# A third buffer for cast q, one input buffer fewer, and a new split of one ReLU stage

## The chip, the cores and the metric

The kernel runs on one core of a Trainium2 chip. The core has a matrix engine (TensorE, PE in the profile), a vector engine (VectorE, DVE), a scalar engine (ScalarE, ACT), a general engine (GpSimd, POOL), and a sync engine (SyncE, SP), which here only issues DMA transfers. Each engine works off its own queue in order; engines wait for one another through semaphores. PEld is TensorE's loading of weights, which runs beside its matmuls. The metric is the time of one execution on the device in microseconds (us), lower is better. Where several runs are given, the median is meant.

## The reference

The input is q, k, v of 4 batches, 8 heads, 768 positions and 64 numbers per head. Two layers follow each other. The first is a linear attention with a decaying state; the second mixes by two Fourier transforms, normalizes, and applies a two-layer ReLU network:

```python
for t in range(S):
    state = gamma * state + outer(k[:, :, t], v[:, :, t])
    y[:, :, t] = scale * q[:, :, t] @ state
X = fft(fft(x, axis=1), axis=2)
u = x + real(X)
un = (u - mean(u)) / sqrt(var(u) + 1e-6)
out = u + relu(un @ w_ch1) @ w_ch2     # 512 -> 2048 -> 512
```

Here x is y with its heads side by side: 768 rows of 512 numbers for each batch.

## The kernel before

**Attention.** Heads go in pairs, and the four pairs of a batch are taken in turn as i = 0 to 3 (the list `PAIR_ORDER` says which heads these are). `load_unit` issues three loads per pair from SP, for q, k and v, each into one tile of the pool `inp`, which has 11 buffers (line 159 is the load). A load into a buffer that has been used waits until that buffer's last reader is done. `cast_unit` turns them to 16 bits. In batches 0 and 1 q is cast by POOL into the first half of a padded buffer `q16z`, and TensorE transposes it. In batches 2 and 3 (`b >= NPE`) ACT casts q with two copies (line 374), one for each head of the pair, into `q16z`, whose other places hold zeros; then SP issues a DMA transpose of the whole buffer into `qTz` (line 541), beside another of k into `kT` (line 543). Two buffers `q16z` are used in turn, `qzs[i % 2]`: a cast for pair i has to wait until the transpose of the pair that last used that buffer has landed. POOL casts k and v (lines 376 and 381) in all batches. `pad_unit` writes the zeros of `q16z` on DVE during batch 1's attention (lines 253 and 254). After the transposes come the products of q and k (`wkA`, line 593, masked on DVE, line 596), those of k and v (`wkK`, line 612, and the running state `s`, lines 618 and 622), and y (`wkY`, lines 643 and 647), which ACT scales into `x` (line 655).

**Mixing.** The Fourier transforms are matmuls with tables of sines and cosines. Their last step is `s2_unit`, once for each block `kb` of 128 rows, six in a batch. It is a chain over four engines: TensorE makes `pq` (line 826), ACT copies two parts of it into `qn` (lines 828 and 829), DVE makes the two halves of `u` (lines 833 and 836), POOL adds `x` to both (lines 863 and 865), DVE takes the statistics (lines 882 and 883), and ACT makes `un` (line 884). `un` is transposed into `unT`, in the later batches by DMA (line 909).

**The network.** For each half `rt` of a batch's rows (384 rows, three blocks), `h_unit` makes 16 blocks `fb` of the hidden layer: four matmuls into one PSUM buffer `psh` (line 929), which ACT (line 933) or DVE (line 935) then empties into `ht` with a ReLU. The list `ACT_ROWS` says for each half which blocks ACT empties. Afterwards `ch_unit` makes the output: 16 matmuls for each 128 rows into `psc` (line 972), one DVE instruction (line 976) and a store from SP (line 980). `psh` and `psc` share one PSUM pool with three buffers, so the matmuls of block fb can start only when block fb-3 has been emptied.

**The order.** The network of batch b is written interleaved with the attention of batch b+1 and with the mixing of the second half of batch b and of the first half of batch b+1: `emit` sorts all these units by due times. Blocks kb 3 to 5 of a batch's mixing therefore fall into the first ReLU stage of the same batch. The order of the first batch is pinned by hand. Behind that, a scheduler in the kernel framework puts each engine's instructions in line, by what it takes to be ready, and inserts the waits that the buffers need; it may put an instruction that is written later ahead of one written earlier on the same engine.

Of the kernel before, what the change touches and what calls it, by code (L numbers as in the profile page):

```python
# [14 lines left out]
f16 = mybir.dt.float16  # L15
# [3 lines left out]
P = 128  # L19
B, H, S, D = 4, 8, 768, 64  # L20
DM = 512
DFF = 2048
NCH = S // P
# [7 lines left out]
ON_ACT = {'q': (0, 1, 0), 'kv': (1, 1, 1), 'g': (0, 1, 1), 'gr': (0, 0, 0)}  # L31
FB = 1
NPE = 2
ACT_ROWS = ((2, 4, 5, 6, 7, 8, 9, 10, 14), (0, 3, 6, 7, 9, 10, 11, 12, 14, 15))


@with_exitstack
def kernel(
# [13 lines left out]
    def pool(name, bufs, **kw):  # L52
        return ctx.enter_context(tc.tile_pool(name=name, bufs=bufs, **kw))

    const = pool("const", 1)
    inp = pool("inp", 11)
    vp = pool("vp", 4)
    kp = pool("kp", 3)
    tp = pool("tp", 2)
# [189 lines left out]
                                scalar2=1.0, op0=ALU.mult, op1=ALU.mult)  # L249

    def pad_unit():
        for j in range(2):
            nc.vector.memset(qzs[j][:, 0, :, D:P], 0.0)
            nc.vector.memset(qzs[j][:, 1, :, 0:D], 0.0)

# [65 lines left out]
        return run  # L321


    xts, qns, qzs, qts = [], [], [], []
    for j in range(2):
        x = const.tile([P, NCH, 2, XW], f16, tag=f"x16_{j}", name=f"x16_{j}")
        xts.append(x)
        qz = const.tile([P, 2, NCH, P], f16, tag=f"q16z_{j}", name=f"q16z_{j}")
        qzs.append(qz)
        qt = const.tile([P, 2, NCH, P], f16, tag=f"qTz_{j}", name=f"qTz_{j}")  # L330
        qts.append(qt)
        t = const.tile([P, 257], f32, tag=f"qn_{j}", name=f"qn_{j}", padded_shape=[P, 260])
        nc.gpsimd.memset(t[:, 0:257:256], 0.0)
        qns.append(t)
# [18 lines left out]
    at, q16_of, kd_of, v16_of, last_cast = {}, {}, {}, {}, {}  # L353

    def cast_unit(b, i):
        def run():
            h0 = 2 * PAIR_ORDER[i]
            q32, k32, v32 = (in_of.pop((n, b, i)) for n in "qkv")
            kd = kp.tile([P, NCH, 2, D], f16, tag="kd16", name="kd16")
            v16 = vp.tile([P, NCH, 2, D], f16, tag="v16", name="v16")  # L360
            with ExitStack() as es:
                if b < NPE:
                    if (b, i - 1) in last_cast:
                        es.enter_context(tc.issue_after(last_cast[b, i - 1].ins))
                    q16 = qzs[i % 2].rearrange("p h c d -> p (h c d)")[
                        :, 0:NCH * P].rearrange("p (c h d) -> p c h d", c=NCH, h=2)
                    es.enter_context(tc.issue_after(nc.gpsimd.tensor_scalar(
                        out=q16, in0=q32.rearrange("p h c d -> p c h d"), scalar1=1.0,
                        scalar2=1.0, op0=ALU.mult, op1=ALU.mult).ins))
                else:  # L370
                    q16 = qzs[i % 2]
                    for h2 in range(2):
                        dst = q16[:, h2, :, D * h2:D * h2 + D]
                        nc.scalar.copy(dst, q32[:, h2])
                for h2 in range(2):
                    kc = nc.gpsimd.tensor_scalar(out=kd[:, :, h2, :], in0=k32[:, h2],  # L376
                                                 scalar1=gkd[:, h0 + h2:h0 + h2 + 1],
                                                 scalar2=1.0, op0=ALU.mult, op1=ALU.mult)
                    if b < NPE:
                        es.enter_context(tc.issue_after(kc.ins))  # L380
                last_cast[b, i] = nc.gpsimd.tensor_scalar(  # L381
                    out=v16, in0=v32.rearrange("p h c d -> p c h d"), scalar1=1.0, scalar2=1.0,
                    op0=ALU.mult, op1=ALU.mult)
            q16_of[b, i], kd_of[b, i], v16_of[b, i] = q16, kd, v16
        return run

    def q0_unit(i):
        def run():
            q16 = q16_of[0, i] = qzs[i % 2].rearrange("p h c d -> p (h c d)")[
                :, 0:NCH * P].rearrange("p (c h d) -> p c h d", c=NCH, h=2)  # L390
            nc.gpsimd.tensor_scalar(out=q16, in0=in_of.pop(("q", 0, i)).rearrange(
                "p h c d -> p c h d"), scalar1=1.0, scalar2=1.0, op0=ALU.mult, op1=ALU.mult)
        return run
# [530 lines left out]
    def h_unit(b, rt, fb):  # L924
        def run():
            unT = lb[b]["unT"]
            psh = ps_pm.tile([P, 384], f32, tag="pm", name="psh", padded_shape=[P, DM])
            for cb in range(4):
                nc.tensor.matmul(psh, w116[:, cb, fb * P:(fb + 1) * P],  # L929
                                 unT[:, cb, rt * 384:(rt + 1) * 384],  # L930
                                 start=(cb == 0), stop=(cb == 3))
            if fb in ACT_ROWS[rt]:
                nc.scalar.activation(ht16[:, fb, :], psh, AF.Relu, bias=0.0, scale=-1.0)  # L933
            else:
                nc.vector.tensor_scalar(out=ht16[:, fb, :], in0=psh, scalar1=-1.0, scalar2=0.0,  # L935
                                        op0=ALU.mult, op1=ALU.max)
        return run
# [239 lines left out]
```

## Time and profile before

| | |
|---|---|
| median of 5 runs | 248.72 us (248.57 to 251.57) |
| the profiled execution: time on the device | 248.6 us |
| its span, first instruction to last | 246.6 us |
| TensorE matmul busy | 234.4 us, 95% of the span |
| DVE busy | 176.4 us, 72% |
| ACT busy | 130.6 us, 53% |
| POOL busy | 73.3 us, 30% |
| granted TensorE clock | 1.0 |

The profile records one execution. Busy time is the time in which an engine had an instruction under way; the rest of the span it stood idle. The timeline lists an engine's instructions in order of time, with the start and the length in us, instructions of one kind that follow each other merged (x3 means three), and in brackets the idle time ahead of an instruction and who ended it. The list of waits adds such idle times up by who waited for whom. "To landing" is the time from the issue of a DMA to the arrival of its last byte. The span and the 2.0 us around it make up the 248.6 us.

### The profile page before, as it was taken

How to read it: one execution, taken by the hardware profiler on the slowest of the kernel's cores; microseconds unless marked ns; L12 is line 12 of the kernel's file. 1: busy time of each engine (PE TensorE's matmuls, PEld its weight loads, DVE VectorE, ACT ScalarE, POOL GpSimd, SP SyncE). 2: the span in 40 equal slices, each digit the busy share in tenths (PEclk: the TensorE clock that was granted, in tenths of full speed). 3: DMA queues.
4: the chain of work that ended last, by engine and by line, in shares of the span. 5: the costliest groups of instructions: out<-in, count | busy, mean ns of one | idle time of the engine just before them, and what ended most of it. 6: DMA issues, size and time to landing. Idle time of an engine off the chain costs nothing.

```text
span 246.6 us, 5310 instructions
## 1 busy us (share of the span) xinstructions
PE 234.4 (95%) x2024; PEld 144.4 (59%) x2024; DVE 176.4 (72%) x427; ACT 130.6 (53%) x295; POOL 73.3 (30%) x130
## 2 busy tenths in 40 slices
PE   6998899999999999999999999799999998999994
PEld 2455578856775645765567456465666455545543
DVE  8998957898788786996985739687895656424112
ACT  8798678487786447862248427742247317202500
POOL 6667500395500074650001707520002304000000
PEclk9999999999999999999999999999999999999999
DMA  8999999799999288989999579494200241221012
GB/s 179 261 256 145 203 196 205 171 247 254 278 214 213 51 170 196 197 151 143 239 272 219 105 168 202 100 148 114 84 1 0 49 148 21 45 85 43 0 45 85
DMA packets 99209, 36.39 MB, mean 148 GB/s; under 512 B 89840, under 2 KB 96240, under 8 KB 99184
## 3 DMA queue, kind: packets, MB, share of 16 engines
q1 hardware_dynamic: 94960, 31.86, 62.6%
q0 software_dynamic: 4224, 4.19, 10.7%
q8 instruction: 16, 0.26, 0.5%
q14 instruction: 9, 0.07, 0.1%
HBM read 27.26 MB, written 6.29 MB: 136 GB/s over the span
## 4 chain that ended last, share of the span: by engine, by line
PE 72%; ACT 9%; DVE 5%; DMA 4%; SPq 3%; POOL 3%; issue 2%; ACTq 0%; DVEq 0%
PE psc L972 30%; PE psh L929 24%; PE ps L729 3%; SPq L159 3%; PE psh L946 3%; PE wkA L593 3%; DMA k<-in_k_dram 2%; DMA qTz<-q16z 2%; PE wkY L647 2%; ACT un L884 1%; PE wkY L643 1%; PE wkK L612 1%; PE pq L826 1%; POOL u L865 1%; DVE bst L882 1%
## 5 line engine op out<-in xcount | busy, mean ns | idle before, releaser
L972 PE MATMUL psc<-w,ht 128*128 128x512 f16 (+1 forms) x400 | 89.8, 371 | 0.0
L929 PE MATMUL psh<-unT,w 128*128 128x384 f16 x448 | 82.1, 326 | 2.4 <-ACT ht L933 2.3
L972 PEld LDWEIGHTS <-ht 128*128 128x128 f16 x400 | 38.0, 98 | 35.0
L929 PEld LDWEIGHTS <-w 128*128 128x128 f16 x448 | 42.2, 98 | 26.2 <-issue 3.4
L933 ACT ACTIVATE ht<-psh 128x384 f16<-128x384 f32 x67 | 31.9, 489 | 37.2 <-PE psh L929 36.2
L863 POOL TENSOR_TENSOR u<-u,x 128x256 f32<-128x256 f32 x21 | 13.3, 635 | 110.5 <-DVE u L833 100.1
L976 DVE SCALAR_TENSOR_TENSOR ob<-psc,stats,u 128x512 f32<-128x512 f32 (+1 forms) x25 | 18.0, 721 | 26.2 <-PE psc L972 26.1
L935 DVE TENSOR_SCALAR ht<-psh 128x384 f16<-128x384 f32 x45 | 24.7, 550 | 8.7 <-PE psh L929 8.2
L596 DVE TENSOR_TENSOR atm<-wkA,maskp 128x512 f16<-128x512 f32 x36 | 23.9, 682 | 1.0 <-PE wkA L593 1.0
L884 ACT ACTIVATE un<-u,stats 128x512 f16<-128x512 f32 x21 | 15.2, 723 | 15.2 <-DVE stats L883 10.9
L882 DVE BATCH_NORM_STATS2 bst<-u 128x6 f32<-128x512 f32 x21 | 14.6, 694 | 8.9 <-POOL u L865 8.8
L622 DVE SCALAR_TENSOR_TENSOR s<-s,gk,wkK 128x128 f16<-128x128 f16 x48 | 16.4, 342 | 2.5 <-ACT s L618 1.4
L655 ACT ACTIVATE x<-wkY,gexp 128x384 f16<-128x384 f32 x24 | 12.9, 584 | 8.3 <-PE wkY L647 8.3
L145 PE MATMUL wps<-ht 128*128 128x512 f16 x40 | 13.5, 444 | 2.2 <-POOL ht L196 2.2
L376 POOL TENSOR_SCALAR kd<-k,gexp 128x384 f16<-128x384 f32 x24 | 13.8, 588 | 2.2 <-DMA k<-in_k_dram 2.2
L865 POOL TENSOR_TENSOR u<-u,x 128x256 f32<-128x256 f32 x21 | 13.3, 636 | 3.6 <-DVE stats L883 1.8
L593 PE MATMUL wkA<-qTz,kT 128*128 128x256 f16 x72 | 13.6, 273 | 0.1
L828 ACT COPY qn<-pq 128x128 f32<-128x128 f32 x18 | 4.9, 273 | 12.9 <-PE pq L826 12.9
L946 PE MATMUL psh<-unT,w 128*128 128x128 f16 x192 | 11.5, 219 | 0.1
L946 PEld LDWEIGHTS <-w 128*128 128x128 f16 x192 | 11.0, 98 | 0.7 <-issue 0.5
L833 DVE SCALAR_TENSOR_TENSOR u<-pq,g,qn 128x256 f32<-128x256 f32 x18 | 8.5, 474 | 3.2 <-ACT qn L829 2.9
L381 POOL TENSOR_SCALAR v<-v 128x768 f16<-128x768 f32 x12 | 10.0, 830 | 2.2 <-DMA v<-in_v_dram 2.2
(164 smaller groups left out, 316.1 us busy)
## 6 DMA issues: line engine op xcount, KB each, us to landing
q<-in_q_dram SPq DMA_DIRECT2D x16, 384.0 KB, 6.3
k<-in_k_dram SPq DMA_DIRECT2D x16, 384.0 KB, 5.7
v<-in_v_dram SPq DMA_DIRECT2D x16, 384.0 KB, 6.0
out_dram<-ob SPq DMA_DIRECT2D x23, 256.0 KB, 2.5
w<-in_moe_w_ch_dram POOLq DMA_DIRECT2D x8, 512.0 KB, 11.0
out_dram<-ob SPq DMA_DIRECT2D x2, 128.0 KB, 1.7
unT<-un SPq DMA_TRANSPOSE x15, 2.4
kT<-kd SPq DMA_TRANSPOSE x8, 3.0
```

Of the source, the lines that this page charges most:

```text
L593: mm = nc.tensor.matmul(wk[:, c2], st["kT"][:, c, :], st["qT"][:, :, c, :], start=True, stop=True)
L596: nc.vector.tensor_tensor(out=st["atm"][:, 2 * part:2 * part + 2], in0=wk, in1=maskp[:, PAIR_ORDER[i]].unsqueeze(1).to_broadcast([P, 2, 2, ...
L622: nc.vector.scalar_tensor_tensor(out=s16[:, c], in0=s16[:, c - 1], scalar=gk2[:, hp:hp + 1], in1=wk[:, c - c0], op0=ALU.mult, op1=ALU.add)
L865: nc.gpsimd.tensor_tensor(out=u[:, kb, 256:512], in0=u[:, kb, 256:512], in1=x[:, kb, 1, 257:1:-1], op=ALU.add)
L882: nc.vector.bn_stats(bst, u[:, kb, :])
L884: una = nc.scalar.activation(un, u[:, kb, :], AF.Identity, bias=stats[:, kb, 0:1], scale=-1.0)
L929: nc.tensor.matmul(psh, w116[:, cb, fb * P:(fb + 1) * P], unT[:, cb, rt * 384:(rt + 1) * 384], start=(cb == 0), stop=(cb == 3))
L933: nc.scalar.activation(ht16[:, fb, :], psh, AF.Relu, bias=0.0, scale=-1.0)
L935: nc.vector.tensor_scalar(out=ht16[:, fb, :], in0=psh, scalar1=-1.0, scalar2=0.0, op0=ALU.mult, op1=ALU.max)
L946: mm = nc.tensor.matmul(psh[:, f], w116[:, cb, fb * P:(fb + 1) * P], unT[:, cb, kb * P:(kb + 1) * P], start=(cb == 0), stop=(cb == 3))
L972: nc.tensor.matmul(psc[:, c0:c1], ht16[:, fb, rb3 * P:(rb3 + 1) * P], w216[:, fb, c0:c1], start=(fb == 0), stop=(fb == NFB - 1))
L976: nc.vector.scalar_tensor_tensor(out=ob[:, c0:c1], in0=psc[:, c0:c1], scalar=lb[b]["st"][:, rb, 3:4], in1=lb[b]["u"][:, rb, c0:c1], op0=AL ...
```

## The change

Three things change.

- `q16z` exists three times instead of twice, and pair i uses buffer i % 3: pairs 0 and 3 share buffer 0, pair 1 has buffer 1, pair 2 has buffer 2. All three are padded.
- The pool of input tiles has 10 buffers instead of 11. One such buffer and one `q16z` buffer are of the same size, 3 KB in each partition.
- In the first half of the last batch ACT empties blocks 2, 4, 6, 8, 10, 12 and 14 instead of 2, 4, 5, 6, 7, 8, 9, 10 and 14, and DVE the others.

```diff
-ACT_ROWS = ((2, 4, 5, 6, 7, 8, 9, 10, 14), (0, 3, 6, 7, 9, 10, 11, 12, 14, 15))
+ACT_ROWS = ((2, 4, 5, 6, 7, 8, 9, 10, 14), (0, 3, 6, 7, 9, 10, 11, 12, 14, 15), (2, 4, 6, 8, 10, 12, 14))
...
-    inp = pool("inp", 11)
+    inp = pool("inp", 10)
...
     def pad_unit():
-        for j in range(2):
+        for j in range(3):
...
+    qzs = [const.tile([P, 2, NCH, P], f16, tag=f"q16z_{j}", name=f"q16z_{j}") for j in range(3)]
...
-                    q16 = qzs[i % 2].rearrange("p h c d -> p (h c d)")[
+                    q16 = qzs[i % 3].rearrange("p h c d -> p (h c d)")[
...
-                    q16 = qzs[i % 2]
+                    q16 = qzs[i % 3]
...
-            q16 = q16_of[0, i] = qzs[i % 2].rearrange("p h c d -> p (h c d)")[
+            q16 = q16_of[0, i] = qzs[i % 3].rearrange("p h c d -> p (h c d)")[
...
-            if fb in ACT_ROWS[rt]:
+            if fb in ACT_ROWS[2 if (b, rt) == (B - 1, 0) else rt]:
```

More of the change, by code (lines that the diff above doesn't have):

```diff
@@ L321, in t_act @@
         return run
-    xts, qns, qzs, qts = [], [], [], []
+    xts, qns, qts = [], [], []
+    qzs = [const.tile([P, 2, NCH, P], f16, tag=f"q16z_{j}", name=f"q16z_{j}") for j in range(3)]
     for j in range(2):
@@ L327 @@
         xts.append(x)
-        qz = const.tile([P, 2, NCH, P], f16, tag=f"q16z_{j}", name=f"q16z_{j}")
-        qzs.append(qz)
         qt = const.tile([P, 2, NCH, P], f16, tag=f"qTz_{j}", name=f"qTz_{j}")
```

## The prediction

> **What bounds the kernel now.** The page first: engines' busy time, and the chain that ended last.
>
> ```profile
> PE 234.4 (95%) x2024; PEld 144.4 (59%) x2024; DVE 176.4 (72%) x427; ACT 130.6 (53%) x295; POOL 73.3 (30%) x130
> ...
> PE 72%; ACT 9%; DVE 5%; DMA 4%; SPq 3%; POOL 3%; issue 2%; ACTq 0%; DVEq 0%
> ```
>
> TensorE is the bound: 12.2 us of the 246.6 are not its own. The change adds and removes no matmul, so it can only win idle time of TensorE, or add some. Next the list of what TensorE waited for (whole span), which shows how little of that is in reach:
>
> ```profile
> PE psh L929 <- ACT ht L933: 2.3, 3, 1.6
> PE wps L145 <- POOL ht L196: 2.2, 1, 2.2
> ```
>
> Three waits for ACT to empty a ReLU block, 2.3 us in all, are the largest sum; the other idle time lies in the first 40 us, which the change hardly touches, and in the drain at the end. The timeline places the three. One, 1.64 us long, is in the stage where batch 2's first ReLU half, its mixing blocks 3 to 5 and batch 3's casts run together:
>
> ```profile
> 145.17 1.46 SPq L541 DMA_TRANSPOSE qTz<-q16z  x1
> ...
> 148.08 0.28 ACT L828 COPY qn<-pq 128x128 f32<-128x128 f32 x1 [4.81 <-PE pq L826]
> ...
> 150.06 1.58 SPq L541 DMA_TRANSPOSE qTz<-q16z  x1
> ...
> 152.22 1.23 ACT L933 ACTIVATE ht<-psh 128x384 f16<-128x384 f32 x3
> ...
> 155.51 0.51 ACT L374 CAST q16z<-q 128x384 f16<-128x384 f32 x1 [2.06 <-DMA qTz<-q16z]
> ...
> 157.21 0.81 PE L929 MATMUL psh<-unT,w 128*128 128x384 f16 x4 [1.64 <-ACT ht L933]
> ```
>
> ACT stood 2.06 us in front of a cast that needed a buffer whose transpose (issued at 150.06) had not landed; block 8's ReLU was queued behind, and TensorE, three PSUM buffers ahead, ran dry. The other two waits are in the last batch's first ReLU half, 0.21 us ahead of block 8 and 0.44 us ahead of block 11:
>
> ```profile
> 206.36 2.11 PE L929 MATMUL psh<-unT,w 128*128 128x384 f16 x12 [0.21 <-ACT ht L933]
> ...
> 208.91 3.41 PE L929 MATMUL psh<-unT,w 128*128 128x384 f16 x20 [0.44 <-ACT ht L933]
> ```
>
> So the change aims at 1.64 + 0.65 = 2.29 us. Whether it gets them is read from the order of the instructions that the scheduler made of either version, engine by engine.
>
> **Batch 3's casts.** ACT's order from 142 us on (c0 to c3: the casts of pair 0 to 3, two instructions each; qn: both copies; h: ReLU of a block):
>
> - before: c0, sqrt, qn, h2, c1, s, h4, qn, un, h5 h6 h7, half of c3, qn, half of c3, h8, un, h9, c2, h10
> - after: c0, sqrt, **c3**, qn, h2, c1, s, h4, qn, un, h5 h6 h7, qn, h8, un, h9, c2, h10
>
> The cast that waited was pair 3's, not pair 2's. With i % 3 it shares buffer 0 with pair 0, and the scheduler has moved it up to just behind c0, two places ahead of even pair 1's. It now waits for pair 0's transpose, issued at 145.17, in front of everything else in this stage. Its issue cannot come earlier: SP is busy with transposes and a store that waits for DVE until then. That transpose took this long:
>
> ```profile
> L541 SPq DMA_TRANSPOSE qTz<-q16z x1: 1459/1459/1459, 145.2 to 145.2; - x1
> ...
> DMA to landing us min/median/max: 3.9/3.9/3.9
> ```
>
> It lands at 145.17 + 3.9 = 149.07. ACT, idle since 143.27, starts c3 at 149.16 (0.1 us after a landing, as at 155.51) and comes to the qn copies 0.82 us later, at 149.98 instead of 148.08: 1.90 us late. Steps of the same instructions in the old timeline carry this on; every engine's queue is in order:
>
> - h2 ends 150.79 (was 149.22). Block 5 needs its buffer: TensorE starts it at 150.82 instead of 150.35, 0.47 us idle.
> - DVE's two u instructions stand ahead of h3, so h3 ends at 151.84 instead of 149.94; block 6 starts 151.87, 0.40 us idle.
> - POOL's additions end 152.26, the statistics 153.32, un of block 3 runs 153.49 to 154.21 (was 151.59), and h5, queued behind it, ends 154.61. Block 8 starts 154.64 after 0.80 us idle (block 7, two wkA and pq fill the time to 153.84).
> - From here the old stall of 2.06 us is gone. un of block 4 starts 156.96 (was 157.03), the last u at 156.72 (was 156.39), h8 ends 156.04, h10 at 159.29 (was 159.34). Block 11 starts 157.09 instead of 157.21, block 13 at 159.32 instead of 159.40, the first psc at 161.95 instead of 162.00.
>
> Sum of the stage: -1.64 us, and 0.47 + 0.40 + 0.80 = 1.67 us in its place, less some hundredths: **-0.05 us**. The wait is not removed, it is moved from behind h7 to ahead of h2. The reason the two come out alike is that the chain qn, u, POOL, statistics, un, three times in a row, sets the pace after 148.08, and both versions hold it up once by about 2 us. Behind the stage, c1 is cast 1.9 us later and its transpose of q is issued near 151.6, of k near 153.5; with the 5.3 and 4.3 us that they took they land by 158, and TensorE needs them at 160: hidden. Pair 2's transposes move by 0.35 us; the old one landed at 160.65 + 5.4 = 166.0 and TensorE took it at 166.37, so this cover is just used up.
>
> The Trainium skill (DMA: Bandwidth & Descriptors, Latency and other measured facts) gives a DMA transpose 261 GB/s; as an estimate the 393 KB of one buffer (128 x 12 x 128 numbers of 2 bytes) would take 1.5 us, land before ACT's next work at 148.08, and the sum would be -1.64 us. The row of 3.9 us decides. The same page's rules for kernel authors advise to issue a DMA early and to wait on its semaphore late; the old order does that better here than the new one, which speaks against the change.
>
> **Batch 2's casts.** The same hoist puts c3 between h6 and h7, at 101.0. Its buffer's transpose, issued at 94.86, took 4.5 us and landed at 99.4: no wait. The pair of casts (0.91 us) delays h7 to 102.4 and h8 to 103.3; TensorE started blocks 10 and 11 at 102.53 and 103.46, so 0.15 us of cover is left. Block 13 may lose 0.07 us; the casts that leave the queue at 105.38 and 108.35 let x run earlier, where TensorE idled 0.1 us at 108. Taken as 0; bounds ±0.2.
>
> **One input buffer fewer.** A load now waits for the tile ten loads back, not eleven. In batch 0 the last two loads wait for casts that end by 7.4 us and are issued at 14.43 and 15.02. In batches 1 to 3 the tile in question is cast well before the load's turn (the closest in batch 2: v of pair 3 waits for k of pair 0, cast by 92.8, and is issued at 98.22), except batch 3's k of pair 3: it waits for c0 (143.07), and the scheduler has put it behind the transpose of 145.17. Loads took 4 to 7 us, so it lands by 154; POOL casts it at 160. SP spends 0.5 to 2 us on it before pair 1's transpose, which waits for ACT until 151.6 anyway. Cost 0; if SP were late there, at most 2 us of which TensorE has 2 us of cover.
>
> **Padding.** Two more memsets of 0.22 us on DVE between 55 and 58 us, where DVE idled 0.57 and 0.86 us. Cost 0.
>
> **The last batch's first ReLU half.** DVE's order becomes u u, h5, statistics, h7, u u, h9, statistics, h11, h13, h15. By the old rows: h5 ends 206.28 (ACT: 206.33), block 8 starts 206.31. But h7 is behind the statistics of block 4, which wait for POOL until 206.73: it ends 207.93 (ACT: 207.07), block 10 starts 207.96 after 0.35 us idle. h9 ends 209.28, block 12 idles 0.05. h11 is behind the statistics of block 5 (POOL until 209.70), ends 210.90, block 14 idles 0.32 us and starts 210.93 (was 210.86). Sum: -0.65 + 0.72 = **+0.07 us**. Bounds: -0.65, if nothing waits, and +0.6, if both u pairs come 0.3 us later than reckoned.
>
> **Sum.** -0.05 + 0 + 0 + 0.07, or about 0, on the profiled execution's 248.6 us (246.6 span and 2.0 around it). The median is 0.1 us above that execution: **248.7 us**.
>
> **Rivals.** *The waits really go.* For it: pair 3 now takes the buffer that pair 0 filled 13 us before the old c3, and pairs 1 and 2 wait for nobody. Against: the new order. If pair 0's transpose lands by 147.2, ACT has done c3 by 148.08, and -1.64 us remain, at most -2.29 with the ReLU part: 246.4 to 247.1 us. *The transpose lands late.* ACT is now blocked in front of the whole stage, so each us that pair 0's transpose needs beyond 3.9 us goes to TensorE one for one. The eight transposes took 3.8 to 6.3 us; one with store traffic ahead, the next one, took 5.3. That would be +1.4 us, 250.1; the longest +2.4 us, 251.1. It turns slower than before as soon as it lands after 149.2. *The ReLU split alone decides*: 248.0 to 249.3, inside the forecast.
>
> **Chances.** Forecast (248.0 to 249.4) 0.62; waits gone or half gone 0.14; late landing or handoffs that add up 0.22; else 0.02. The range, 8 in 10: from 247.0 (the large wait gone) to 250.2 (a landing of 5.3 us). One per cent, 2.5 us, is about what a measurement of this kernel can tell from no change. Faster by more would take all of the 2.29 us and more: 0.03. Slower by more needs the longest landing and something beside it: 0.07. Within: 0.90.
>
> **What would show it.** In the changed profile: ACT's longest wait for a transpose ends near 149 instead of 155.4, and is ahead of a qn, not behind h7; three small idle times of TensorE ahead of psh between 150 and 155 in place of one of 1.64; in the last batch psh waiting for DVE's ht twice, about 0.3 us each. No cast waiting at all would prove me wrong on the main step; so would a first psc of batch 2 that starts more than 0.7 us from 162.0.

## The result

The changed kernel is slower by a little. Its median is 249.54 us (54 executions, 248.32 to 251.58), beside 248.99 us of the kernel before (95 executions); the ratio is **1.0027, 95% interval 1.0017 to 1.0038**, or +0.4 to +0.95 us. The ratio is that of the means of the fast executions; three of the kernel before (251.57 to 252.22 us) count as slow and are left out, and the medians alone differ by 0.55 us. The forecast was no change, 248.7 us. The 54 times lie in two groups: 37 below 250.2 us, with a mean of 249.30, and 17 above it, with a mean of 250.73; four of these 17 ran at a mean granted clock of 0.993, all others of the 54 at 0.998 or more. The kernel before has 87 below, with a mean of 249.00, and 8 above.

The profiled execution of the changed kernel took 248.3 us with a span of 246.6, the same span as that of the kernel before. Its line numbers from 330 on are one lower than before (L374 is now L373). Busy time, and the chain that ended last:

```profile
PE 234.2 (95%) x2024; PEld 144.2 (58%) x2024; DVE 177.3 (72%) x431; ACT 130.0 (53%) x293; POOL 73.7 (30%) x130
...
PE 33%; POOL 3%; ACT 2%; DVE 2%; DMA 2%; issue 1%; SPq 1%; POOLq 0%; ACTq 0%
```

The chain can't be set beside the old one: it was followed back only to 137 us, and its shares make up less than half of the span. The list of what TensorE waited for, whole span:

```profile
PE wps L145 <- POOL ht L196: 2.2, 1, 2.2
...
PE psh L928 <- ACT ht L932: 1.0, 3, 0.5
...
PE psh L928 <- DVE ht L934: 0.4, 2, 0.2
```

The three waits for ACT of 2.3 us, 1.6 of them in one piece, have become five short ones of 1.4 us. ACT's timeline in the stage of batch 3's casts shows the hoisted cast of pair 3 and its wait:

```profile
142.27 0.91 ACT L373 CAST q16z<-q 128x384 f16<-128x384 f32 x2
...
149.25 0.93 ACT L373 CAST q16z<-q 128x384 f16<-128x384 f32 x2 [5.87 <-DMA qTz<-q16z]
150.08 0.26 ACT L827 COPY qn<-pq 128x128 f32<-128x128 f32 x1
```

and TensorE's timeline what it lost by it, up to block 11, and in the last batch:

```profile
150.95 0.81 PE L928 MATMUL psh<-unT,w 128*128 128x384 f16 x4 [0.33 <-ACT ht L932]
151.94 0.81 PE L928 MATMUL psh<-unT,w 128*128 128x384 f16 x4 [0.18 <-DVE ht L934]
...
154.64 0.81 PE L928 MATMUL psh<-unT,w 128*128 128x384 f16 x4 [0.50 <-ACT ht L932]
...
157.09 0.81 PE L928 MATMUL psh<-unT,w 128*128 128x384 f16 x4
...
206.29 4.38 PE L928 MATMUL psh<-unT,w 128*128 128x384 f16 x24 [0.21 <-ACT ht L932]
210.85 1.46 PE L928 MATMUL psh<-unT,w 128*128 128x384 f16 x8 [0.18 <-DVE ht L934]
```

The wait of 5.87 us ends at 149.25 (forecast 149.16), qn starts at 150.08 (149.98), TensorE stands idle three times, ahead of blocks 5, 6 and 8, and block 11 starts at 157.09 (157.09). In this execution the stage goes nearly as reckoned. But it is the fastest of the 54. So the question is not what the change does but why the other executions take longer than this one.

### The profile page after: what moved, and what is told of

Its sections match the earlier page's. It is cut to its first block, busy times and chain, and to the rows that moved or that the text cites. A ratio compares the mean times of both kernels' runs of the same rounds, so it can differ in the third digit from the quotient of the medians.

```text
span 246.6 us, 5311 instructions
## 1 busy us (share of the span) xinstructions
PE 234.2 (95%) x2024; PEld 144.2 (58%) x2024; DVE 177.3 (72%) x431; ACT 130.0 (53%) x293; POOL 73.7 (30%) x130
## 5 line engine op out<-in xcount | busy, mean ns | idle before, releaser
L934 DVE TENSOR_SCALAR ht<-psh 128x384 f16<-128x384 f32 x47 | 25.8, 550 | 8.6 <-PE psh L928 8.1
L145 PE MATMUL wps<-ht 128*128 128x512 f16 x40 | 12.6, 420 | 2.2 <-POOL ht L196 2.2
L373 ACT CAST q16z<-q 128x384 f16<-128x384 f32 x16 | 7.3, 508 | 5.9 <-DMA qTz<-q16z 5.9
```

## The experiments

**How stages are compared.** TensorE's queue holds the same 2024 matmuls in nearly the same order in all these kernels. The start of one and the same matmul in two profiles, each from its span's start, can therefore be subtracted, and the difference between two such points is what a stage lost. All losses below are taken so, against the first profile of the kernel before: up to 31 us ("start"), from there to 123 us (nearly all of it near 106 us, "batch 2"), from there to 177 us ("batch 3's casts"), and behind 200 us ("ReLU split").

**1. The parts one by one.** The ReLU split alone (with the new list in `ACT_ROWS`):

```diff
...
-            if fb in ACT_ROWS[rt]:
+            if fb in ACT_ROWS[2 if (b, rt) == (B - 1, 0) else rt]:
```

> The kernel before with the new split of the last batch's first ReLU half alone. By the prediction's sum it is +0.07 us beside the kernel before (ratio 1.000): two waits of 0.65 us in all become three of 0.72. If the ReLU split is what makes the changed kernel 0.6 us slower, the whole of it shows here: about +0.6 us, ratio 1.0024 or more. If the buffers are the cause, at most +0.1 us.

The change without the split:

```diff
...
-            if fb in ACT_ROWS[2 if (b, rt) == (B - 1, 0) else rt]:
+            if fb in ACT_ROWS[rt]:
```

> The changed kernel without the new ReLU split: three padded buffers, ten input buffers, the hoisted casts of pair 3. By the prediction's sum -0.05 us beside the kernel before (ratio 0.9998). If the wait ahead of the whole stage is more sensitive to the landing of pair 0's transpose than the old one behind h7, or if the third buffer costs elsewhere, about +0.6 us, ratio 1.0024 or more, with executions near 250.5 us among them.

The input buffers alone:

```diff
-    inp = pool("inp", 11)
+    inp = pool("inp", 10)
```

> The kernel before with ten input buffers instead of eleven and nothing else; batch 3's load of k of pair 3 stands behind pair 0's transpose. By the prediction 0 us (ratio 1.000). If the missing input buffer is the cause (a late load in the first 30 us, or SP held up ahead of pair 1's transpose), +0.4 to +0.6 us, ratio 1.002.

Measured beside the kernel before on the same chip: the split alone 249.54 us, ratio 1.0029 (1.0006 to 1.0052); the buffers without the split 249.41 us, ratio 1.0001 (0.9974 to 1.0027); the input buffers alone 251.59 us, ratio **1.0100** (1.0070 to 1.0131).

The split's 1.0029 is at odds with its own profile, in which it lost 0.06 us behind 200 us, as forecast (0.07). The last number is the surprise: taking one input buffer away from the old kernel costs 2.5 us. SP's and ACT's timelines of that run's profile, an execution of 249.86 us, show how the first part of it comes about:

```profile
145.90 1.47 SPq L541 DMA_TRANSPOSE qTz<-q16z  x1
147.42 0.87 SPq L159 DMA_DIRECT2D k<-in_k_dram  x1
...
151.43 2.82 SPq L541 DMA_TRANSPOSE qTz<-q16z  x1
```

```profile
157.00 0.51 ACT L374 CAST q16z<-q 128x384 f16<-128x384 f32 x1 [2.84 <-DMA qTz<-q16z]
```

The load of k of pair 3 now stands between the two transposes. The second, which the old order's cast of pair 3 waits for, is issued 0.68 us later than with the split alone (150.75), took 5.5 us, and ACT waits 2.84 us instead of 1.49. The stage takes 0.77 us more than in the first profile of before. The rest of the 2.5 us is not in this profile: in ten of the twelve executions the granted clock was 0.991 to 0.993, and these took 251.2 to 252.8 us; the two at 1.0, the profiled one among them, took 249.7 and 249.9. In the changed kernel nobody waits for pair 1's transpose any more, which is the likely reason that the input buffer's cost does not show there; the changed kernel with eleven input buffers was not run. The parts do not add up.

**2. The order of the casts.** The rule that a pair's cast stands behind the last pair's, in `cast_unit`:

```diff
...
-                        nc.scalar.copy(dst, q32[:, h2])
+                        qc = nc.scalar.copy(dst, q32[:, h2])
+                        if (b, i - 1) in q_cast:
+                            tc.add_manual_dep(qc.ins, q_cast[b, i - 1].ins.name,
...
+                    q_cast[b, i] = qc
```

Put into the changed kernel:

> The changed kernel with one more rule of order: on ACT the cast of q of a pair stands behind that of the pair before. Pair 3's cast is then issued near 159 us in batch 3, when pair 0's transpose landed about 10 us ago, so no cast waits. If the prediction's reason is right (the third buffer does nothing because the order puts pair 3's cast ahead of everything), the qn copies start near 148.1 us again and the idle 1.64 us is gone without the three that replaced it: about -1.6 us beside the kernel before (246.4 to 247.5 us, ratio 0.990 to 0.996). If the ReLU split or the input buffer costs 0.6 us by itself, about -1.0 us. If the pace of the stage is set by something else, 0 us or above, and another wait stands ahead of psh between 150 and 158 us.

Into the kernel before, with its two buffers:

> The kernel before (two padded buffers, eleven input buffers, old ReLU split) with the rule of order alone: on ACT the cast of q of a pair stands behind that of the pair before. Pair 2 then reuses pair 0's buffer near 156.5 us and pair 3 pair 1's near 158 us, when pair 1's transpose (issued near 151, 4.5 to 5.4 us) should have landed about 1 us earlier. If the order of the casts is the whole cause of the idle 1.64 us, this gains as much as the changed kernel with the rule did: -1.6 to -2.0 us beside the kernel before (ratio 0.991 to 0.994), without a third buffer. If the third buffer is needed, pair 3's cast waits again and the gain is under 1 us.

Into the changed kernel with the old split:

> The changed kernel with the rule of order, and with the old ReLU split. Beside the same with the new split (246.96 us, spread only 1.0 us) it tells the ReLU split's own price in a kernel whose executions hardly differ. By the prediction's sum and by three pairs of profiles (+0.06 each) it is 0.06 us faster: about 246.9 us, ratio 0.991. If the split costs the 0.6 to 0.8 us that the run with the split alone showed, about 246.2 us, ratio 0.989.

Measured: 246.96 us, ratio **0.9913** (0.9880 to 0.9946); two buffers 247.62 us, 0.9948 (0.9924 to 0.9971); old split 246.88 us, 0.9924 (0.9904 to 0.9944). ACT's timeline of the first (its line numbers behind the cast are eight higher than in the changed kernel):

```profile
148.60 0.27 ACT L835 COPY qn<-pq 128x128 f32<-128x128 f32 x1 [4.81 <-PE pq L833]
...
156.49 0.91 ACT L374 CAST q16z<-q 128x384 f16<-128x384 f32 x2
...
157.84 0.53 ACT L374 CAST q16z<-q 128x384 f16<-128x384 f32 x1
```

No cast waits, TensorE has no idle time ahead of psh in the stage, and the stage of batch 3's casts takes 2.05, 2.05 and 2.04 us less than in the first profile of before in the three kernels. Two things follow. The wait was a matter of the order, not of the number of buffers: with the right order two buffers remove it just as well. What the two-buffer kernel lacks beside the others lies elsewhere, as far as one profile of each shows it: 0.95 us lost near 106 us, beside -0.02 and 0.52, and 0.2 us around the span. And the seven times of the first kernel lie within 1.0 us, the six of the third within 0.8; the second group of the changed kernel is gone, though pair 0's transpose took 5.0 us in the profile of the first. With and without the new split the medians are 0.08 us apart (measured on two chips, on which the kernel before differed by 0.05 us).

**3. Further executions of both kernels.** Two of each, and one of the kernel with the split alone, were run first, then three of the changed one:

> The changed kernel once more, for the trace of another execution. If the spread of its times comes from the landing of pair 0's transpose in batch 3, the copies of qn start near 150.1 us and the time is about 249.3 us when it lands after 3.9 us, and near 151.2 us and about 250.5 us when it lands after 5.0 us.

> The kernel before with the new ReLU split alone, once more, for the trace of another execution. Its last batch's first ReLU half should again end 0.06 us later than in the kernel before. If the split is dearer in most executions, the time between TensorE's first psh and first psc of that half is longer by 0.5 us or more; if not, what its median has over the kernel before lies in the first 25 us or at the transposes near 106 us and between 150 and 158 us, where the split has no part.

> The kernel before once more, for the trace of another execution. Its first profile is of 246.6 us span, near the low end of its spans. If what the other kernels' profiles lose to it in the first 25 us (0.13 to 0.6 us) and near 106 us (0 to 1.2 us) is chance, it loses some of it here too. If it is their doing, TensorE's matmuls up to 145 us start within 0.1 us of the first profile's. If the old order usually waits less for pair 3's buffer than the first profile showed (there the transpose took 5.35 us and the wait 1.64), the wait ahead of block 8 is near 1.1 us here, as in the two profiles of the kernel with the split alone, where that transpose took 4.8 us.

> As the run above: the kernel before, a further execution, to tell its usual landings from chance.

> The changed kernel, a further execution. If a pause of the DMA engines catches pair 0's transpose, it lands 5.0 us after its issue and TensorE loses about 1 us more between 148 and 158 us than at 3.9 us; otherwise as in the first two profiles, -0.2 us beside the first profile of the kernel before.

> The changed kernel, a further execution. Time near 249.3 us if pair 0's transpose in batch 3 lands about 3.9 us after its issue, near 250.7 us if it lands after 5.0 us or more, with the idle time ahead of psh between 150 and 160 us 1.0 us in the first case and about 2.1 us in the second.

> As the run before it: a further execution of the changed kernel.

> As the run before it: a further execution of the changed kernel.

Two more, meant to tell what a comparison of this length can show by chance: the kernel before against itself, and the split alone again.

> The kernel before, compared with itself. If the comparison has no lean of its own, ratio 1.000, with an interval of about 0.25% to either side, as wide as that of the other runs of this length. A ratio near 1.003 would say that what the changed kernel lost needs no cause in the change.

> The kernel before with the new ReLU split alone, in a second comparison. If the split's price is what its profiles show (+0.06 us), the ratio is 1.000 to 1.001 here; if the 0.29% of the first comparison was real, 1.003 again.

The kernel before against itself gave 0.9989 (0.9960 to 1.0018), the split the second time 0.9974 (0.9950 to 0.9998). The split's two ratios average to 1.000, so its 0.29% is put down to chance. But the two intervals of one and the same kernel do not even meet: the intervals of these shorter comparisons, of twelve executions, are too narrow, and a difference of 0.3% in one of them proves nothing.

The stages of the profiles of both orders, in us beside the first profile of before; the fourth of before and the third of the split alone are from the two comparisons just named. "Transpose" is the time from issue to landing of the one whose landing pair 3's cast awaits in batch 3: pair 1's in the old order, pair 0's in the new.

| profile | start | batch 2 | batch 3's casts | split | transpose |
|---|---|---|---|---|---|
| before, 1st | 0 | 0 | 0 | 0 | 5.35 |
| before, 2nd | 0.79 | 1.15 | 0.05 | 0 | 5.40 |
| before, 3rd | 0.44 | 1.08 | -0.24 | 0 | 5.11 |
| before, 4th | 0.65 | 0.89 | -0.79 | 0 | 4.54 |
| split alone, 1st | 0.25 | 0.44 | -0.56 | 0.06 | 4.78 |
| split alone, 2nd | 0.17 | 1.20 | -0.53 | 0.06 | 4.82 |
| split alone, 3rd | 0.43 | 0.32 | -0.73 | 0.06 | 4.62 |
| **mean, old order** | **0.39** | **0.73** | **-0.40** | | **4.95** |
| after, 1st | 0.13 | -0.01 | -0.18 | 0.06 | 3.86 |
| after, 2nd | 0.41 | 0.40 | -0.04 | 0.06 | 3.84 |
| after, 3rd | 0.24 | 0.61 | -0.04 | 0.06 | 3.91 |
| after, 4th | 0.45 | 0.36 | **1.09** | 0.06 | **5.03** |
| after, 5th | 0.55 | 0.57 | -0.02 | 0.07 | 3.91 |
| after, 6th | 0.63 | 0.86 | -0.01 | 0.07 | 3.89 |
| buffers, old split | 0.52 | 0.26 | **1.10** | 0 | **5.02** |
| **mean, new order** | **0.42** | **0.44** | **0.27** | **0.06** | **4.21** |

Three things are to be read from it. The first profile of before, from which the forecast was made, is the best of the seven in the first 31 us and near 106 us, and the second worst in batch 3's casts. The new order has two cases: five times the transpose took 3.9 us and the stage about as long as in that profile, twice 5.0 us and 1.1 us more. And the old order's stage follows its own transpose: 4.54 us gave -0.79, 5.35 and more gave 0 and 0.05. The old order's wait ahead of block 11, expected near 1.1 us in the further profiles of before, was 1.7, 1.4 and 0.9 us.

The fourth profiled execution of the changed kernel took 250.4 us, so it lies with the upper group; the other five, with landings after 3.9 us, took 248.3 to 249.9. ACT's and TensorE's timelines:

```profile
151.13 0.92 ACT L373 CAST q16z<-q 128x384 f16<-128x384 f32 x2 [7.05 <-DMA qTz<-q16z]
```

```profile
152.82 0.81 PE L928 MATMUL psh<-unT,w 128*128 128x384 f16 x4 [1.51 <-ACT ht L932]
```

Why the landing comes late is seen in the windows of 1 us: the columns at the end are the granted clock, the DMA share and GB/s. The fourth execution:

```profile
147.70:148.70 1.00, 1.00 (x11) 0.68 (x10) 0.92 (x3) 0.00 (x0) 0.00 (x0) 1.00 2.22 214
148.70:149.70 1.00, 1.00 (x10) 0.61 (x8) 0.52 (x1) 0.00 (x0) 0.00 (x0) 1.00 0.44 8
149.70:150.70 1.00, 1.00 (x11) 0.73 (x10) 0.00 (x0) 0.00 (x0) 0.00 (x0) 1.00 0.95 208
```

and the third, with a landing after 3.9 us:

```profile
148.70:149.70 1.00, 1.00 (x10) 0.62 (x8) 0.56 (x1) 0.00 (x0) 0.00 (x0) 1.00 0.98 190
```

For about 1.2 us the DMA engines moved 8 GB/s instead of some 200. Counted by the packets that the trace holds (fewer than 15 begin in 0.1 us, where it is else some 80), such a pause, 0.6 to 1.7 us long and with transfers under way, falls between 148 and 157 us in every one of these profiles; in most of them it comes behind 151 us, and pair 0's transpose has landed by then. In six of the seven profiles of the old order it lies inside pair 1's transpose instead; the two longest pauses there, 1.5 and 1.7 us, go with the two latest landings, after 5.35 and 5.40 us. In the old order the pause is harmless where it catches pair 0's transpose, for which nobody waits yet, and pair 1's then lands sooner: that is before's fourth profile, with 5.06 us for pair 0, 4.54 us for pair 1, and the stage 0.79 us shorter.

In batch 2's stage the changed kernel is the better one by the means (0.44 beside 0.73), though the profiles scatter so much there (0 to 1.2 us) that the 0.29 us could be chance. TensorE's waits between 104 and 112 us in the third profile of before:

```profile
PE wkA L593 <- DMA kT<-kd: 0.5, 1, 0.5
PE wkA L593 <- ACT x L655: 0.5, 1, 0.5
```

and in the third of the changed kernel:

```profile
PE wkA L592 <- DMA kT<-kd: 0.6, 1, 0.6
```

Both wait for a transpose of k that landed late (4.9 and 4.65 us after its issue). In the old order a half of pair 3's cast and an un stand in front of x on ACT, and TensorE waits for x too; in the new order the cast is gone from there and x is made at 105.62 us, ahead of un.

**4. Moving the landing.** Behind the load and the store that followed it:

```diff
...
+                if (b, i) == (B - 1, 0):
+                    tc.add_manual_dep(tr.ins, stores[-1].ins.name,
...
```

> The changed kernel, with SP's transpose of q of pair 0 in batch 3 put behind the load and the store that followed it: issued near 148.4 us instead of 145.3. If the end follows the landing one for one, +3.1 us beside the changed kernel (249.5), about 252.6 us, and ACT's cast of pair 3 starts near 152.3 us. If the stage has slack of its own, less than 2 us. If the landing plays no part, 249.5 us.

Ahead of the store before it (and the load behind the stores):

```diff
...
+                if (b, i) == (B - 1, 0):
+                    tc.add_manual_dep(stores[-2].ins, tr.ins.name,
...
+                if (b, i, name) == (B - 1, 3, "k"):
+                    tc.add_manual_dep(dma.ins, stores[-2].ins.name,
...
```

> The changed kernel, with the same transpose put ahead of the store before it, and the load of k of pair 3 behind both stores: issued near 144.7 us instead of 145.3, with less other traffic. If the end follows the landing one for one, -0.6 us beside the changed kernel, about 248.9 us or a little less, the kernel before's time. If the landing plays no part, 249.5 us.

Measured: late 253.16 us, ratio 1.0144 (1.0110 to 1.0179); early 249.21 us, ratio 0.9980 (0.9949 to 1.0012). The early one again has two groups, six executions from 247.95 to 248.88 us and six from 249.54 to 250.65. Their means, 248.42 and 250.01 us, are 0.88 and 0.72 us below the changed kernel's 249.30 and 250.73, for an issue that came 0.6 us earlier (reckoned, as the next numbers, from the start of the stage). These times were taken in another comparison, in which the kernel before took 249.26 us instead of 248.99, so that the gain is rather more than less. The early kernel's profile, of an execution of 249.57 us, has a landing 0.93 us later than in the five profiles of the changed kernel that had 3.9 us, and a stage 0.90 us longer; in the two profiles with 5.0 us the landing is 1.14 us later and the stage 1.15 us longer. That is one for one. The late transpose was issued 1.4 us later, not 3.1, because the store ahead of it did not wait as expected; the transpose itself then took 6.3 us to land. The landing in its profile is 3.8 us later than in the changed kernel's first, and the stage 5.3 us longer, more than one for one. TensorE's timeline and the windows show the rest (granted clock: third number from the end):

```profile
155.44 2.72 PE L934 MATMUL psh<-unT,w 128*128 128x384 f16 x8 [4.13 <-ACT ht L938]
```

```profile
150.00:155.00 5.00, 1.30 (x14) 0.93 (x13) 0.00 (x0) 1.26 (x5) 0.00 (x0) 0.95 1.27 176
155.00:160.00 5.00, 4.56 (x16) 2.29 (x16) 4.47 (x12) 3.67 (x12) 4.35 (x7) 0.50 0.66 139
160.00:165.00 5.00, 5.00 (x53) 3.49 (x52) 4.10 (x10) 3.66 (x10) 3.15 (x6) 0.86 0.19 37
```

TensorE stood idle for 4.1 us, and got half the clock for about 6.9 us: the last 0.5 us of the first window, the whole second and 1.4 us of the third, as an estimate from the three means. All six executions had a mean clock of 0.986 to 0.993. So the end follows the landing one for one as long as the clock stays; in this run, where it did not, the stage lost 1.5 us more than the landing was late.

## Why the prediction was wrong

**Batch 3's casts (-0.05 us): the term that failed.** The mechanism is right: the cast of pair 3 is hoisted, the wait moves from behind h7 to ahead of h2, and the same chain sets the pace. Each of its steps that the profile after shows came within about 0.1 us. The list gives the three idle times as 0.33, 0.18 and 0.50 us instead of 0.47, 0.40 and 0.80, but it counts from the modelled end of the matmul before; from start to start, as the forecast reckoned them, they are 0.49, 0.34 and 0.66. The sum set them against the list's 1.64 us for the old wait, which from start to start is 1.80, so it mixed two measures; that is worth 0.16 us and did not decide. The size is wrong on both sides, because both were read from one execution. The old wait of 1.64 us was nearly the longest of seven (0.9 to 1.7); on average the old order's stage is 0.40 us shorter than in the profile used. The new side was priced at a landing after 3.9 us, which holds in five profiles of seven; in the other two it is 5.0 us and the stage 1.1 us dearer. The means, -0.40 and +0.27, make **+0.67 us** of this term, with an uncertainty of some 0.25 us from the scatter of seven profiles on either side. That is 0.72 us more than the -0.05 of the forecast: 0.40 us from the old side and 0.32 from the new. The estimate of 1.5 us for the transpose, from the Trainium skill's rate for a DMA transpose alone (DMA: Bandwidth & Descriptors, Latency and other measured facts; the page states it for a non-contiguous middle dimension), was far from every landing here (3.7 to 6.9 us in all profiles). The advice in the same page's Rules for kernel authors, to wait for a DMA late, is what these runs bear out, since the old order, which waits behind h7, is the better one, and the order that casts pair 3 last the best.

**The rival "the transpose lands late"** had the mechanism, the place and, with "one for one", the price: two of the seven profiles of the new order show it. How often it happens is less sure. By their times up to 17 of the 54 executions had a late landing, but four of these had the lower clock as well, and of the twelve executions with the buffers and the old split only one took more than 250.2 us. The rival's mistake was to be weighed as an alternative for the whole kernel, at 0.22, instead of as a share of the executions that enters the expected time. 1.1 us in two profiles of seven is worth 0.31 us in their mean. A landing could be seen to vary in the profile of before already: eight transposes of one size took 3.8 to 6.3 us.

**Batch 2's casts (0, bounds -0.2 to 0.2):** -0.3 us by the table, with an uncertainty of 0.2. The forecast names the cause (x runs earlier) but took TensorE's 0.1 us of idle time there in the one profile for all there was to gain; in the others the old order lost up to 0.5 us to x.

**One input buffer fewer (0) and padding (0):** no loss from the input buffer shows in the profiles beside the hoisted cast; without that cast it cost 2.5 us. That SP's delay ahead of pair 1's transpose is covered was right for the new order. Padding could not be told from nothing: between 31 and 106 us, where its memsets lie, the old order lost 0.01 us on average and the new 0.04.

**The ReLU split (+0.07):** +0.06 or +0.07 in each of the twelve profiles that have it, and 0.08 us between two kernels whose times hardly scatter.

**Around the span (2.0 us in both):** 1.75 us in the changed kernel (median of 54), 1.96 in the kernel before (median of 29). The forecast took it as fixed; this is 0.2 us in favour of the change.

**The sum.** 0.03 + 0.67 - 0.29 + 0.06 makes +0.47 us of span, less 0.2 around it, +0.27 us. Measured are +0.67 us (0.42 to 0.95). From the scatter of the columns, seven profiles against seven leave an uncertainty of some 0.4 us, so the two do not contradict each other; but 0.4 us have no place found for them, and stay open. The range (247.0 to 250.2) and the 0.90 for "within 1%" hold; the narrower forecast (248.0 to 249.4) was missed by 0.14 us.

## What to carry to other kernels

When an engine's queue hangs on a DMA's landing, a single profile gives one sample of it: take the price from several landings of that transfer, and put a late one into the sum with its share, not beside it as a rival. Before adding a buffer, look where in the queue the instruction stands that waits for it: here an order of four casts gained 0.8 to 0.9% with the third buffer and 0.5% without it (the intervals overlap), while the third buffer in the order that the scheduler chose gained nothing. An edit that shows no cost beside another one can cost 1% alone, so parts measured singly need not add up to the whole.

## What the runs showed of the hardware

- Nearly all DMA engines stopped together for 0.6 to 1.7 us (8 GB/s beside some 200 in the fourth execution of the changed kernel) with transfers under way, between 148 and 157 us in each of these profiles, but not at the same transfer each time. What causes it was not tried.
- TensorE's granted clock fell to 0.50 for about 6.9 us, as an estimate from three windows, around the end of 4.1 us without work. An idle time of 2.4 us left it at 1.0 in the profile with ten input buffers alone, but ten of that kernel's twelve executions had a mean clock of 0.991 to 0.993 and took 1.3 us or more longer than the two others; that these had the same dip was not seen in a profile.
- The time around the span had medians of 1.7 to 1.8 us in all kernels with ten input buffers and of 1.9 to 2.0 us in those with eleven; single executions reach from 1.7 to 1.9 and from 1.7 to 2.1 us. Why was not tried.
